# Cutting a weight load into pieces by rows: three uneven cuts taken away, one other cut put in

## The chip, the cores and the metric

The kernel runs on one core of one Trainium2 chip. The metric is the device time of one execution in microseconds; lower is better. Three executions of the kernel before took 427.69, 428.08 and 428.46 us, so the median is 428.08 us. A further execution was recorded by the hardware profiler; what is said below about engines, waits and transfers comes from that one.

## The reference, cut to what matters

The kernel computes sparse causal attention and then mixes its output in the frequency domain. In short:

```
attn = softmax(mask(q k^T / 8)) v          # 8 batches, 8 heads, 576 positions, 64 columns
x = attn, heads side by side                # [8, 576, 512]
X = rfft(x along the positions), modes 0..63
Yr = X.re @ w_r[m] - X.im @ w_i[m]          # one 512 x 512 complex matrix for each mode m
Yi = X.re @ w_i[m] + X.im @ w_r[m]
u = x + irfft(Y)
out = u + relu(u @ w_ch)                    # float32
```

The matrices w_r and w_i are float32 [64, 512, 512]: 64 MB each. Every element of them is read from memory once and used for 8 batches only. The page counts 162.83 MB read from memory in all.

## The kernel before, in words

**The stream of weights.** The work is cut along the 512 input columns into two halves of 256, and the modes are taken in pairs. One *fetch* brings, for one half and two neighbouring modes, the real part (256 rows of w_r for two modes, 1 MB of float32) into partitions 0 to 63 of a tile and the imaginary part (the same of w_i) into partitions 64 to 127. Each of the two is one DMA, issued by POOL, that converts float32 to float16 on its way: 64 rows (partitions) x 2 modes x 2048 numbers. In the profile it is `DMA_DIRECT2D wt<-in_moe_w_r_dram` or `...w_i_dram` on line 186, 512 KB as written.

`ORDER` (lines 150 and 151) lists 128 pairs (half, mode); entry i with even i stands for a fetch, so there are fetches i = 0, 2, ... 126. I call a fetch by i and its two DMAs 62r and 62i, 64r and 64i, and so on. The last two fetches (124 and 126) are made of four DMAs each, one for each part and mode (line 190, 256 KB as written).

**Pieces.** `UNEVEN` (line 152) names fetches whose real part is not one DMA of 64 rows but several of fewer rows, in the order given, over neighbouring partitions (lines 179 to 184; the issue is on line 182). Before, fetch 64 is cut into 25, 12 and 27 rows, fetch 80 into 6, 54 and 4, and fetch 96 into 10 and 54. The imaginary part is always whole. The total of bytes is the same with any cut.

**What orders the transfers.** The schedule is written out by hand (`manual_schedule`), so the instructions of each engine run in the order of the program. `w_fetch` is called where a mode pair has been used (lines 607 and 637), and its DMAs go on POOL's queue. The tiles come from a pool of five (`NWBUF`, line 27), so a fetch also waits until the matmuls of the pair five fetches back are done. In the list of POOL's instructions, its DMAs take one of eight semaphores in turn, and each waits for the DMA that used the same semaphore last, eight DMAs earlier. So up to eight of POOL's DMAs are under way at a time.

**What uses the weights.** `mode_pair` (lines 585 to 612, matmuls on line 597) multiplies by a pair once both its parts have landed. The last 16 modes of half 0 go through `mode` (lines 614 to 647, matmuls on line 630), one mode at a time, between pieces of other work: `renew` (lines 948 to 961), which folds spectra that are done into rows that were kept. When mode 127 of the order has been used, the last spectra are turned (lines 1042 to 1053) and the rows of the output are made and written (lines 1056 to 1081); nothing of that can start earlier for the last spectra.

**The stages.** From 0 to about 95 us the strided heads' attention runs beside loads of q, k and v; from about 95 to 195 us the local heads' attention runs between the first mode pairs of half 1; from about 195 us on there are only mode pairs, the product with w_ch and the turns of the attention output beside them; from about 392 us on all inputs are there and the output is made.

Of the kernel before, what the change touches and what calls it, by code (L numbers as in the profile page):

```python
# [56 lines left out]
def kernel(  # L57
# [91 lines left out]
    SPLIT1, SPLIT0 = 56, 48  # L149
    ORDER = [(1, m) for m in range(SPLIT1)] + [(0, m) for m in range(SPLIT0)]  # L150
    ORDER += [(1, m) for m in range(SPLIT1, NM)] + [(0, m) for m in range(SPLIT0, NM)]
    UNEVEN = {64: (25, 12, 27), 80: (6, 54, 4), 96: (10, 54)}
    w_tiles = []
    w_chs = {}
    w_ch = big.tile([128, 4, DM], F16, name="w_ch")
# [1 line left out]
    def w_fetch(n=1):  # L157
        for _ in range(n):
# [9 lines left out]
            for ri, src in enumerate((moe_w_r, moe_w_i)):  # L168
# [8 lines left out]
                if ri and not m:  # L177
                    ones = [1]
                elif i in UNEVEN and not ri:
                    a = 0  # L180
                    for n in UNEVEN[i]:
                        nc.gpsimd.dma_start(dst[a : a + n], rows[a : a + n])
# [930 lines left out]
```

## Time and profile before

| what | value |
|---|---|
| three executions, median (lowest to highest) | 428.08 us (427.69 to 428.46) |
| profiled execution, first to last instruction | 426.7 us |
| what the median has on top of that span | 1.4 us |
| busy: PE / DVE / ACT / POOL | 81% / 55% / 51% / 26% of the span |
| packets of POOL's DMAs, share of 16 DMA engines' time | 96.2% |
| 512 KB weight DMAs, median from issue to landing | 18.8 us (w_i), 17.7 us (w_r) |
| the eight pieces on line 182, issued | 218.3 to 300.0 us, 15.3 to 19.0 us to landing |
| last weight DMA issued, landing | 382.3 us, 9.6 us later |

How it is read: the page gives busy shares over the whole span, but a share near 100% says which resource is full, not which part of it ends last. The 16 DMA engines work side by side, each on its own share of every DMA, and a DMA has landed only when the last of them is done with it. The trace keeps a record of each packet (start, duration, size, queue), so one can also ask how far apart the 16 engines are. The chain of waits, followed back from the end, says which of all this the end waited for.

### The profile page before, as it was taken

How to read it: one execution, taken by the hardware profiler on the slowest of the kernel's cores; microseconds unless marked ns; L12 is line 12 of the kernel's file. 1: busy time of each engine (PE TensorE's matmuls, PEld its weight loads, DVE VectorE, ACT ScalarE, POOL GpSimd, SP SyncE). 2: the span in 40 equal slices, each digit the busy share in tenths (PEclk: the TensorE clock that was granted, in tenths of full speed). 3: DMA queues.
4: the chain of work that ended last, by engine and by line, in shares of the span. 5: the costliest groups of instructions: out<-in, count | busy, mean ns of one | idle time of the engine just before them, and what ended most of it. 6: DMA issues, size and time to landing. Idle time of an engine off the chain costs nothing.

```text
span 426.7 us, 9768 instructions
## 1 busy us (share of the span) xinstructions
PE 346.4 (81%) x4167; PEld 208.2 (49%) x4167; DVE 234.7 (55%) x466; ACT 218.3 (51%) x390; POOL 110.7 (26%) x196
## 2 busy tenths in 40 slices
PE   2977878769999698889768788878788867889993
PEld 2866767554656365566433344435444423445330
DVE  3788778851355154356113246746676354655884
ACT  1687678643656356556642235423442444443872
POOL 8332333322423222222222322222232222210000
PEclk9999899967999689999995889989999979989997
DMA  8999999999999999999999999999999999995698
GB/s 150 210 212 212 213 213 213 211 211 211 214 213 213 213 213 215 212 214 215 210 214 211 213 214 213 210 213 215 212 213 214 213 213 214 214 212 105 244 355 287
DMA packets 30938, 91.62 MB, mean 215 GB/s; under 512 B 4464, under 2 KB 5232, under 8 KB 30896
## 3 DMA queue, kind: packets, MB, share of 16 engines
q0 software_dynamic: 25168, 81.28, 96.2%
q1 hardware_dynamic: 4976, 9.13, 5.9%
q10 hardware_dynamic: 752, 0.61, 0.5%
q8 instruction: 32, 0.52, 0.5%
q14 instruction: 10, 0.08, 0.0%
HBM read 162.83 MB, written 9.44 MB: 404 GB/s over the span
## 4 chain that ended last, share of the span: by engine, by line
DMA 47%; PE 29%; DVE 14%; ACT 5%; issue 3%; DVEq 0%; POOL 0%; ACTq 0%; POOLq 0%
DMA wt<-in_moe_w_i_dram 38%; DMA wt<-in_moe_w_r_dram 7%; PE y L597 5%; DVE xb L241 3%; DVE kz L283 3%; PE p L987 2%; ACT X L251 2%; PE sc L532 2%; PE tp L413 2%; PE sc L459 1%; PE p L1001 1%; PE y L532 1%; PE p L760 1%; DVE yy L752 1%; DVE rec L240 1%
## 5 line engine op out<-in xcount | busy, mean ns | idle before, releaser
L597 PE MATMUL y<-wt,X 128*32 128x512 f16 (+1 forms) x448 | 70.9, 430 | 20.1 <-DMA wt<-in_moe_w_i_dram 20.1
L186 POOL DMA_DIRECT2D wt<-in_moe_w_r_dram x59 | 34.7, 588 | 126.4 <-PE y L597 56.3
L186 POOL DMA_DIRECT2D wt<-in_moe_w_i_dram x60 | 35.4, 590 | 68.3 <-DMA wt<-in_moe_w_i_dram 44.4
L597 PEld LDWEIGHTS <-X 128*32 128x32 f16 (+1 forms) x448 | 28.1, 140 | 39.4 <-DMA wt<-in_moe_w_i_dram 18.6
L727 DVE COPY xo<-tp 128x512 f16<-128x512 f16 x32 | 22.1, 691 | 36.8 <-PE tp L725 36.8
L726 ACT ACTIVATE v<-sc 128x512 f16<-128x512 f32 x32 | 19.1, 597 | 44.2 <-PE sc L717 44.2
L717 PE MATMUL sc<-w_cp,xT 128*128 128x512 f16 x128 | 36.9, 410 | 1.9 <-DVE xT L690 1.9
L489 ACT ACTIVATE PL<-sc 128x480 f16<-128x480 f32 (+1 forms) x48 | 27.0, 578 | 21.3 <-PE sc L475 21.0
L241 DVE TENSOR_TENSOR xb<-av,rec 90x256 f16<-90x256 f32 (+2 forms) x80 | 36.0, 450 | 2.8
L240 DVE RECIPROCAL rec<-av 90x4 f32<-90x4 f32 (+2 forms) x80 | 14.6, 183 | 39.3 <-PE av L504 28.2
L251 ACT ACTIVATE yr<-y 128x512 f16<-128x512 f32 x28 | 16.7, 597 | 36.8 <-PE y L597 35.6
L961 DVE TENSOR_TENSOR xo<-p,xo 128x1024 f16<-128x1024 f32 x16 | 19.6, 1225 | 21.7 <-PE p L760 21.7
L420 DVE COPY qT<-tp 128x576 f16<-128x576 f16 x16 | 11.9, 752 | 34.7 <-PE tp L413 34.7
L251 ACT ACTIVATE v<-p 128x1024 f16<-128x1024 f32 x16 | 16.4, 1023 | 23.1 <-PE p L760 23.1
L378 ACT ACTIVATE PL<-sc 90x360 f16<-90x360 f32 (+1 forms) x48 | 22.7, 490 | 7.0 <-PE sc L371 6.4
L251 ACT ACTIVATE v<-tp 128x640 f16<-128x640 f16 (+1 forms) x24 | 19.0, 807 | 11.8 <-PE tp L447 9.3
L413 PE MATMUL tp<-cI_s,ring 64*64 64x64 f16 x864 | 22.4, 197 | 2.7 <-DVE qT L420 2.4
L459 PE MATMUL sc<-cMl_s,cI_s 128*128 128x480 f16 (+1 forms) x48 | 19.4, 405 | 4.5 <-ACT PL L489 2.9
L276 PE MATMUL tp<-cI_s,ring 72*128 72x72 f16 x256 | 15.4, 207 | 8.7 <-DMA ring<-in_v_dram 7.1
L413 PEld LDWEIGHTS <-ring 64*64 64x64 f16 x864 | 17.5, 110 | 9.4 <-issue 5.4
L251 ACT ACTIVATE kz<-tp 64x360 f16<-64x360 f16 (+1 forms) x32 | 18.9, 592 | 6.2 <-PE tp L413 5.2
L1013 ACT ACTIVATE rl<-p 128x1024 f32<-128x1024 f32 (+1 forms) x19 | 18.4, 979 | 5.7 <-PE p L1001 3.1
(142 smaller groups left out, 737.9 us busy)
## 6 DMA issues: line engine op xcount, KB each, us to landing
wt<-in_moe_w_i_dram POOLq DMA_DIRECT2D x60, 512.0 KB, 18.8
wt<-in_moe_w_r_dram POOLq DMA_DIRECT2D x59, 512.0 KB, 17.7
out_dram<-osb SPq DMA_DIRECT2D x15, 512.0 KB, 3.4
ring<-in_v_dram POOLq DMA_DIRECT2D x8, 288.0 KB, 13.4
ring<-in_q_dram POOLq DMA_DIRECT2D x8, 288.0 KB, 13.6
ring<-in_k_dram POOLq DMA_DIRECT2D x8, 288.0 KB, 13.1
ring<-in_v_dram POOLq DMA_DIRECT2D x3, 512.0 KB, 14.8
ring<-in_q_dram POOLq DMA_DIRECT2D x3, 512.0 KB, 14.8
```

The lines of the kernel that those rows point to most:

```text
L186: nc.gpsimd.dma_start(dst, rows)
L241: nc.vector.tensor_tensor(out=dst, in0=val.rearrange("p h (q c) -> p h c q", c=4), in1=rec[0:n, 0:pieces] .to_broadcast((n, pieces, 64)) . ...
L251: nc.scalar.activation(out=out, in_=in_, func=ACTF.Copy)
L378: nc.scalar.activation(out=PS[0:n, ds(POFF[t], 4 * n)], in_=scp[0:n, 0 : 4 * n], func=ACTF.Exp, scale=SCALE,)
L413: nc.tensor.transpose(tp[ds(64 * hp, 64), ds(64 * i, 64)], qn[ds(64 * hp, 64), ds(64 * (9 * g + i), 64)], idn[ds(64 * hp, 64), ds(64 * hp, ...
L459: nc.tensor.matmul(scp[:, 0 : n * times].rearrange("p (h x) -> p h x", h=times), idn, mask_rows("cMl", n, times), start=True, stop=False,)
L489: nc.scalar.activation(out=dst, in_=src, func=ACTF.Exp, scale=SCALE)
L597: nc.tensor.matmul(yp[ds(a, 32), :], Xh[half][pr, c].rearrange("p b r (h m) -> p (b r h) m", h=2)[:, :, mm % 32], wt[pr, XC[c], :], start= ...
L717: nc.tensor.matmul(vp, xT[:, ch], w_chs["cp"][:, ch, :], start=(ch == 0), stop=(ch == 3),)
L726: nc.scalar.activation(out=v0, in_=vp, func=ACTF.Copy)
L727: nc.vector.tensor_copy(out=xo.rearrange("p (h q c) -> p h q c", h=2, c=4), in_=tp[:, 0:512].rearrange("p (h c q) -> p h q c", h=2, c=4),)
L961: nc.vector.tensor_tensor(out=xo, in0=up[:, 0:n], in1=xo, op=AluOp.add)
```

## The change

The dictionary `UNEVEN` is replaced. Fetches 64, 80 and 96 (half 0, modes 8, 24 and 40) are no longer cut: the real part of each becomes one DMA of 64 rows on line 186. Fetch 98 (half 0, modes 42 and 43), the next after 96, has its real part cut into five DMAs of 15, 14, 13, 12 and 10 rows.

```diff
     ORDER += [(1, m) for m in range(SPLIT1, NM)] + [(0, m) for m in range(SPLIT0, NM)]
-    UNEVEN = {64: (25, 12, 27), 80: (6, 54, 4), 96: (10, 54)}
+    UNEVEN = {98: (15, 14, 13, 12, 10)}
     w_tiles = []
```

POOL's queue has one row fewer: eight pieces become three whole DMAs, and one whole DMA becomes five pieces. As all later DMAs of POOL take their semaphores in turn, those get other numbers. The order of the instructions of PE, ACT, DVE and SP stays as it was, but for the semaphores they wait on.

## The prediction

> **What bounds the kernel now.** I read the page's slices first, then the chain of waits, then the timeline where the last weights arrive, then the packet records.
>
> ```profile
> DMA  8999999999999999999999999999999999995698
> ...
> q0 software_dynamic: 25168, 81.28, 96.2%
> ...
> DMA wt<-in_moe_w_i_dram 38%; DMA wt<-in_moe_w_r_dram 7%; PE y L597 5%; DVE xb L241 3%; DVE kz L283 3%; PE p L987 2%; ACT X L251 2%; PE sc L532 2%; PE tp L413 2%; PE sc L459 1%; PE p L1001 1%; PE y L532 1%; PE p L760 1%; DVE yy L752 1%; DVE rec L240 1%
> ```
>
> The DMA row stands at 9 until slice 36, so POOL's queue (96.2%) keeps all 16 DMA engines at work until the inputs are in; and 45% of the chain that ended last are weight DMAs. Next, the chain in order of time, near the last weights:
>
> ```profile
> 337.54 19.90 DMA wt<-in_moe_w_i_dram
> 357.44 0.28 issue
> 357.73 19.38 DMA wt<-in_moe_w_i_dram
> 377.10 0.14 issue
> 377.24 0.64 PE y L630 x16
> ```
>
> The DMA issued at 357.73 (120i) lands at 377.1 and PE starts 0.14 us later. After that PE is the chain, mode after mode, up to the last:
>
> ```profile
> 391.87 0.59 PE L992 MATMUL p<-xo,cI_s 128*128 128x512 f16 x2
> 392.09 0.73 PEld L630 LDWEIGHTS <-wt 128*128 128x128 f16 x16
> 392.31 0.64 PE L630 MATMUL y<-X,wt 128*128 128x16 f16 x16
> ```
>
> The last weight DMA is issued at 382.31 and lands 9.6 us later, at 391.9; PE loads from it at 392.09. So at the end transfer and PE arrive within 0.2 us of each other. What follows (392.3 to 426.7) is made of work that starts there. The end therefore moves with the moment at which the *slowest* DMA engine is done with the weights.
>
> **How far apart the engines are.** The packet records have no engine number, but POOL's packets follow each other without a gap: the next 4 KB packet starts 305 ns after the last, and at the end of each DMA an engine writes a 4 B packet, which costs 21 ns. A whole DMA is 8 packets on each engine; one engine's 4 B packets come 2457.5 ns apart (1239 ns for the last eight DMAs, of 4 packets). 16 such sequences can be followed from 225 us to the end. Each moves only where an instruction fetch (16 KB, queue q8) takes the engine for about 1.1 us, or an 8 KB one for 0.33 us. Their last 4 B packets come at 386.0 to 391.6 us, 389.4 in the mean: the slowest engine is 2.2 us behind the mean.
>
> The pieces of before show how rows go to engines. A piece runs on the largest number of engines up to 16 that divides its rows: 25 rows on 5 engines (10 packets each), 12 on 12 (2), 27 on 9 (6), 54 on 9 (12), 6 on 6, 4 on 4, 10 on 10 (2). Each piece begins at the engine after the last one of the piece before, around the ring of 16. An engine that has no rows writes as many 4 B packets as the others have data, 6 ns each. Numbering the engines from the first of the 25-row piece, the three cut DMAs together give an engine this many packets, where 24 would be even. "62i done" is the last moment that the change cannot touch; "end" is the last 4 B packet; the last two columns are worked out below.
>
> ```
> engines  packets  62i done (us)             end, before (us)          shift   end, after
> 0        26       229.1                     387.2                     -0.75   386.5
> 1-4      30       228.8 229.3 230.5 231.2   388.1 390.0 390.1 391.6   -1.95   386.2 388.0 388.2 389.7
> 5,6      22       231.8 232.4               389.0 390.4               +0.44   389.4 390.9
> 7,8      32       228.8 229.3               388.8 389.2               -2.55   386.2 386.7
> 9        22       231.5                     389.9                     +0.44   390.3
> 10-12    18       231.8 232.8 233.3         388.7 390.1 390.8         +1.64   390.3 391.7 392.4
> 13-15    18       229.5 232.8 233.0         386.0 389.7 390.2         +1.64   387.6 391.3 391.8
> ```
>
> (Which row a sequence belongs to follows from its packets in the three cut DMAs; within a row the order is by 62i.) What is to be seen: engines 10 to 15 are the late ones at 62i (mean 232.2, against 229.8 for 0 to 4), and the cuts of before give just them 6 packets fewer.
>
> **The change, part by part.**
>
> *Whole real parts for 64, 80, 96.* Every engine then has 24 packets there. Shift of an engine: packets x 304.6 ns, less its empty 4 B packets (22, 18, 26, 16, 26, 30, 30 down the table; about 2 after) x 6 ns, less 21 ns for one DMA fewer. Engines 10 to 15: 6 x 304.6 = +1.83, -0.17, -0.02: +1.64 us. Engines 7 and 8: -8 x 304.6 = -2.44, -0.08, -0.02: -2.55 us.
>
> *Five pieces for 98.* By the same two habits 15, 14, 13, 12 and 10 rows take 15, 14, 13, 12 and 10 engines with one row (2 packets) each. They are 64 places on a ring of 16: 4 for every engine, 8 packets, as from a whole DMA. So this cut shifts nobody; its four more DMAs (4 x 21 ns, at most 0.1 us) are already in the shift.
>
> *Last engine.* From the table the latest end goes from 391.61 (an engine of 1-4) to 390.81 + 1.64 = 392.45 (one of 10-12): **+0.84 us**. Lower bound: that engine's clean time is 233.33 at 62i + 59 whole DMAs (145.0) + the cut one (2.56) + eight short ones (9.91) = 390.8; it came 1.68 us late at 94i, of which a 16 KB fetch at 277.5 explains about 1.1; the other 0.5 falls in 271 to 278 us, where the cut of fetch 80 was being written and many packets took 330 to 570 ns instead of 324. If that goes with the cut, the last end is some 391.9, **+0.25 us**. I take +0.84, the measured delay of the same engine, since the fetch itself took 1.2 us there and nothing shows that the empty packets caused the rest.
>
> *End of the kernel.* 120i lands 0.84 later and PE begins at 378.1 instead of 377.24. From 377.55 to 380.97 the granted clock is 0.5; PE loses 0.31 us at full and 0.55 at half speed, 0.6 in all, so the mode before the last is done at some 393.1 instead of 392.5. The last DMA lands at 392.7 instead of 391.9, so PE's load moves from 392.09 to 392.8: +0.75 us at the last mode. All after it follows. Span 426.7 + 0.75 = 427.4; the median has 1.4 us on top of the span: **428.9 us**.
>
> *Costed at nothing.* POOL's issues: 0.59 us for a whole DMA, 0.57 to 0.71 for a piece, one fewer in all; they are hidden because a DMA is issued 15 to 19 us ahead of its landing. Semaphores: five pieces take five of the eight places, so fewer bytes are queued behind them. When the slowest engine ends 94i it has 96r, 96i and the pieces ahead, 3 x 2.46 = 7.4 us, and 98i is issued then; an engine ahead by 5.8 to 6.5 us (307.4 against 313.2 to 313.9 by the table) may run dry for about a microsecond, but it has 5 us to spare and is not the one waited for. Without that cover each microsecond of dry queue would be one at the end. PE's waits before 392 us: its pairs wait on two parts as before; at 94i the slowest engine would be up to 0.9 us earlier (no heavy cut yet behind it), but PE waits for weights again and again from 342 to 377 us (1.2 to 2.9 us each), so that is lost.
>
> *A rule against the rows.* The trace shows engines taking the next DMA's packet 21 ns after the last. The Trainium skill, "DMA: Bandwidth & Descriptors", section "Anatomy of one DMA", gives about 2.0 us fixed for each DMA on this path. By that, one DMA fewer would be -2 us; with eight under way this trace shows no such cost in the stream. The same page, "Why a DMA increments its semaphore by 16 and not by 1", tells the divisor rule that the pieces show, but also an exception by which 100 partitions go on engines 0 to 14, each copy starting at 0. By the exception the five pieces would give ten engines 10 packets and one none, up to +0.6 us on a late engine, 429.5 in all; the pieces of before don't follow it.
>
> **Rivals.**
>
> 1. *Balance lost, tail follows* (forecast): 428.9; with the bounds 428.3 to 429.0 from the DMA alone.
> 2. *The loss is no loss* (no change): the 0.5 us went with the bursts of empty packets, and PE's half-clock stretch swallows the rest: +0.1 to +0.3, 428.3. For it: packets of 500 to 570 ns around the bursts. Against: 391.8 of another engine stays.
> 3. *Instruction fetches fall elsewhere* (faster). Three of the four latest engines owe 1.1 us each to one fetch after 235 us (298.6, 317.7, 332.6), the fourth the one at 277.5. If the new order of POOL's rows moves them to engines that have time, the last end is 390.8, -0.8 us: 427.2. It decides once all four are spared, since any one of them left is over 391.3. Against: PE, ACT and DVE have the same instructions in the same order, and fetches follow from those.
> 4. *Clock* (slower still). Half-clock stretches come in steps of 3.41 us. The chain from 392 to 419 has PE pieces of 0.54 between others and no such stretch; one there, or a longer one at 377, adds up to 1.7 us: 430.5.
> 5. *Not what it says*: pieces of 15, 14, 13 rows are not in the trace; if they don't follow the ring, a late engine gets up to 10 packets instead of 8: +0.6, 429.5.
>
> **How the numbers follow.** Chances: forecast 0.50, rival 2 0.18, rival 3 0.16, rival 4 0.10, rival 5 0.06. A measurement of this kernel can tell about 0.2% from no change, 0.86 us (427.2 to 428.9). The forecast sits on the upper edge; a little over two thirds of it I count as over, since a later 120i moves work behind it that I have counted at half clock. Slower: 0.35 + 0.10 + 0.05 = 0.50; same: 0.15 + 0.15 + 0.02 = 0.32; faster: 0.15 and 0.03 from rival 2, 0.18. The range takes in rival 3 with 0.2 us below it and rival 4 but for its far end: 427.0 to 430.2.
>
> **What would show it.** Right: 94i's 4 B packets no later than before, but a spread of the last 4 B packets of over 6 us (5.6 before), the last at 392.0 to 392.5; five pieces of 2 packets on 15, 14, 13, 12, 10 engines; 120i landing at 377.4 to 378. Wrong: a last landing at or before 391.9; engines with other than 8 packets in 98r; a chain that doesn't go through 120i or the last DMA.

## The result, and the profile after

| | runs | median (lowest to highest), us |
|---|---|---|
| before, on the same chip | 22 | 427.96 (427.29 to 429.16) |
| changed | 22 | 428.56 (428.02 to 430.55) |

The ratio is 1.0018, 95% interval 1.0011 to 1.0026. The kernel is 0.6 us slower by its medians. The prediction said 428.9, and slower by about 0.8. The profiled execution of the changed kernel took 428.65 us, its span is 426.9.

The page of the changed kernel, the lines that answer to those of before (slices of the DMA engines, POOL's queue, the chain that ended last by line):

```profile
DMA  8999999999999999999999999999999999995698
...
q0 software_dynamic: 24800, 81.28, 96.1%
...
DMA wt<-in_moe_w_i_dram 47%; PE y L597 5%; DMA wt<-in_moe_w_r_dram 4%; PE p L987 2%; PE p L1001 1%; DVE yy L752 1%; PE sc L717 1%; PE sc L459 1%; PE p L992 1%; PE tp L413 1%; PE y L532 1%; PE sc L475 1%; ACT X L251 1%; PE u L992 1%; PE av L496 1%
```

The DMA engines are as full as before, digit for digit, and the bytes are the same; 368 packets are gone, and all of them are 4 B packets (384 empty ones in the three old cuts against 32 in the new one, and 16 fewer at the end of a DMA). Weight DMAs are now 51% of the chain against 45%. The chain in order of time says why (start us, us, what):

```profile
357.28 19.45 DMA wt<-in_moe_w_i_dram
376.73 0.28 issue
377.01 12.33 DMA wt<-in_moe_w_i_dram
389.34 0.14 issue
389.48 0.64 PE y L630 x16
390.11 1.51 PE p L987 x4
391.62 0.85 PE p L992 x2
392.47 0.49 PE y L630 x16
```

Before, the chain left the DMAs at 377.1 and was nearly all PE from there on. Now it follows one more weight DMA, which lands at 389.34. PE's timeline around it, in the changed kernel (start us, us; in brackets the idle time ahead of the row and what ended it):

```profile
389.48 0.64 PE L630 MATMUL y<-X,wt 128*128 128x16 f16 x16 [0.94 <-DMA wt<-in_moe_w_i_dram]
389.95 1.67 PE L987 MATMUL p<-v,cI_s 128*128 128x512 f16 x4
391.41 1.06 PE L992 MATMUL p<-xo,cI_s 128*128 128x512 f16 x2
392.26 0.68 PE L630 MATMUL y<-X,wt 128*128 128x16 f16 x16
```

The last mode is multiplied at 392.26; before, in the profile that the prediction read, at 392.31. So in this pair of executions the last mode came no later, though the medians differ. What comes behind it does: the two matmuls of line 992 take 1.06 us instead of 0.59, because the stretch in which TensorE's clock is granted at half speed (0.5) now lies at 390.2 to 393.6 us (before at 377.6 to 381.0).

Of the fourteen profiles in this document these two alone have a half-speed stretch between 370 and 420 us. In eleven of the other twelve the chain comes to the last mode through the last weight DMA. This is its end in a kernel without any cut (no_cut, below):

```profile
382.21 9.63 DMA wt<-in_moe_w_i_dram
391.84 0.14 issue
391.97 0.65 PE y L630 x16
```

The exception is a second profile of the kernel before (before_again), in which PE itself comes last. Its last mode is multiplied at 391.73 us; without a cut that happens at 391.97 and 392.01, in the two further profiles of the changed kernel at 391.99 and 392.50.

**One profile is one draw.** In 227 of 232 runs the time stood 1.73 to 2.08 us above the span (median 1.79 of all); the other five, 2.4 to 3.0 us above it, are all of one kernel, old_and_five. The span of before has a median of 426.1 us over the 87 runs that were made beside the experiments, and the profiled execution of 426.7 was among the slowest fifth. The changed kernel's median span is 426.7 over 45 runs. So the two profiles differ by 0.2 us where the medians differ by 0.6, and half a microsecond can't be read from one pair of traces. The packet records, which show where each DMA engine stands, are more use.

In the records of the changed kernel the last 4 B packet of POOL's DMAs comes at 391.54 us (before 391.61). The 16 engines end in two groups: eight at 387.3 to 388.5, eight at 390.0 to 391.5. Before they were spread from 386.0 to 391.6.

### The profile page after: what moved, and what is told of

Its sections match the earlier page's. It is cut to its first block, busy times and chain, and to the rows that moved or that the text cites. A ratio compares the mean times of both kernels' runs of the same rounds, so it can differ in the third digit from the quotient of the medians.

```text
span 426.9 us, 9766 instructions
## 1 busy us (share of the span) xinstructions
PE 344.6 (81%) x4167; PEld 207.2 (49%) x4167; DVE 234.8 (55%) x466; ACT 218.3 (51%) x390; POOL 109.8 (26%) x195
## 4 chain that ended last, share of the span: by engine, by line
DMA 52%; PE 19%; DVE 4%; ACT 2%; issue 2%; POOL 0%; DVEq 0%; ACTq 0%
DMA wt<-in_moe_w_i_dram 47%; PE y L597 5%; DMA wt<-in_moe_w_r_dram 4%; PE p L987 2%; PE p L1001 1%; DVE yy L752 1%; PE sc L717 1%; PE sc L459 1%; PE p L992 1%; PE tp L413 1%; PE y L532 1%; PE sc L475 1%; ACT X L251 1%; PE u L992 1%; PE av L496 1%
## 5 line engine op out<-in xcount | busy, mean ns | idle before, releaser
L597 PE MATMUL y<-wt,X 128*32 128x512 f16 (+1 forms) x448 | 69.3, 422 | 21.2 <-DMA wt<-in_moe_w_i_dram 20.9
L186 POOL DMA_DIRECT2D wt<-in_moe_w_r_dram x61 | 35.8, 588 | 132.5 <-PE y L597 41.2
```

The lines of the kernel that those rows point to most:

```text
L186: nc.gpsimd.dma_start(dst, rows)
L597: nc.tensor.matmul(yp[ds(a, 32), :], Xh[half][pr, c].rearrange("p b r (h m) -> p (b r h) m", h=2)[:, :, mm % 32], wt[pr, XC[c], :], start= ...
```

## The experiments

Each kernel is the one before with line 152 alone changed. Runs were made in three groups, each with runs of the kernel before on the same chip (medians 427.79, 427.94 and 428.03 us). The first is before_again, no_cut, old_and_five and more_for_late; the second after_again, four_even, many_even and less_for_late; the third no_cut_b, after_c, five_early and two_fives. "Last packet" is the last 4 B packet of POOL's DMAs in the profiled execution. "Lost" is what is left over of the 180 us between 200 and 380 us, as a mean over the 16 engines, when each packet is counted at its usual length (305 ns for 4 KB); it is good for differences between kernels.

| line 152 | median us (runs) | ratio, 95% interval | span | last packet | lost us |
|---|---|---|---|---|---|
| as before (before_again) | 427.99 (12) | 1.0006, 0.9997 to 1.0016 | 426.2 | 391.25 | 0.4 |
| no cut (no_cut) | 428.22 (12) | 1.0007, 0.9999 to 1.0016 | 426.5 | 391.51 | 0.4 |
| no cut (no_cut_b) | 428.30 (12) | 0.9997, 0.9981 to 1.0013 | 426.5 | 391.55 | 0.4 |
| as changed (after_again) | 428.29 (11) | 1.0014, 1.0003 to 1.0024 | 426.3 | 391.56 | 1.0 |
| as changed (after_c) | 428.40 (12) | 1.0002, 0.9988 to 1.0016 | 427.0 | 392.06 | 0.9 |
| old cuts and the five pieces (old_and_five) | 428.31 (12) | 1.0016, 1.0003 to 1.0028 | 426.2 | 391.38 | 0.9 |
| four equal pieces at 98 (four_even) | 428.92 (11) | 1.0019, 1.0009 to 1.0030 | 427.1 | 392.05 | 0.6 |
| four equal pieces at 90 to 100 (many_even) | 429.81 (6) | 1.0038, 1.0025 to 1.0052 | 428.5 | 393.79 | 3.5 |
| five pieces at 66 instead (five_early) | 428.66 (12) | 1.0005, 0.9992 to 1.0019 | 427.0 | 392.09 | 1.5 |
| five pieces at 82 and 98 (two_fives) | 428.70 (12) | 1.0008, 0.9993 to 1.0022 | 427.0 | 392.17 | 1.1 |
| more rows for the late engines (more_for_late) | 431.19 (6) | 1.0073, 1.0059 to 1.0087 | 428.7 | 393.82 | 1.2 |
| fewer for the late ones (less_for_late) | 429.45 (5) | 1.0031, 1.0019 to 1.0043 | 427.9 | 392.97 | 0.3 |

The third group's intervals are wide (its 35 runs of before reach from 427.3 to 430.9), so the small differences are read from all runs together. Before: 427.94 (121 runs). No cut: 428.25 (24). Changed: 428.53 (45). The differences of these medians, with intervals from resampled runs: no cut less before +0.31 us (0.21 to 0.47), changed less no cut +0.27 us (0.02 to 0.43), changed less before +0.59 us (0.34 to 0.76). The runs come from several chips, which these intervals don't count. Chip by chip, no cut is 0.43 and 0.27 us above the runs of before beside it, the changed kernel 0.60, 0.35 and 0.37. Only the third chip ran both: there the changed kernel is 0.10 us above no cut (-0.24 to 0.47).

### The two halves of the change

before_again changes nothing:

```diff
     UNEVEN = {64: (25, 12, 27), 80: (6, 54, 4), 96: (10, 54)}
```

> The kernel before once more, for a second profile of it. Both theories: ratio 1.000, within 0.0007. Theory of balance: the engines' last 4 B packets again spread over 5 to 6 us, the last one at 391 to 392 us, and the time of the profiled execution moves with the last one (about 1 us for 1 us). Theory of the small pieces: says nothing of it.

It came out at 427.99 us, 1.0006 (0.9997 to 1.0016), as expected. Its engines end at 386.0 to 391.2 us, another order of the same spread: the last packet of one and the same program moves by 0.4 us from one profile to another. This is the yardstick for everything below.

no_cut, and later no_cut_b, take the old cuts away and put none in:

```diff
-    UNEVEN = {64: (25, 12, 27), 80: (6, 54, 4), 96: (10, 54)}
+    UNEVEN = {}
```

> No fetch is cut. Theory of balance (where the rows go sets the time, cutting itself is free): as the changed kernel, 1.0010 to 1.0026 of before, since 15+14+13+12+10 rows give every engine the same. Theory of the small pieces (five small DMAs hold five of the eight places, the queue runs dry behind them, and that is the loss): no loss, 0.999 to 1.0005 of before.

> No fetch is cut, beside the changed kernel and two others. Theory A (the small DMAs of a cut cost time of their own, because they take places among the eight that may be under way, so that fewer bytes are queued and the engines that are ahead run dry): 1.0004 to 1.0012 of the time of before, and below the changed kernel by 0.2 to 0.5 us. Theory B (the five pieces cost nothing; all that the change costs is the balance that the old cuts gave): the same as the changed kernel within 0.15 us.

The first, at 1.0007, lies between the ranges of its two theories. The second, at 0.9997 in the group with the wide intervals, lies below all of them; it is 0.10 us under the changed kernel beside it, which is what theory B asked for (within 0.15 us), but the interval of -0.24 to 0.47 doesn't shut out theory A (0.2 to 0.5). Together they are 0.31 us slower than before. The last packets of the two profiles agree (391.51 and 391.55), and the engines end in two groups, as in the changed kernel: without the old cuts, eight of them stay, in the mean, 3 to 4 us behind the other eight to the end. So the old cuts were worth something, but about 0.3 us. That these 0.3 us are the last engine's isn't seen directly: the last packets, two profiles each, are 0.1 us apart (mean 391.53 without a cut, 391.43 before), less than the 0.4 us by which those of one program differ.

old_and_five keeps the old cuts and puts the five pieces in beside them:

```diff
-    UNEVEN = {64: (25, 12, 27), 80: (6, 54, 4), 96: (10, 54)}
+    UNEVEN = {64: (25, 12, 27), 80: (6, 54, 4), 96: (10, 54), 98: (15, 14, 13, 12, 10)}
```

> The three cuts of before and the five pieces at fetch 98. Theory of balance: as before, 0.9993 to 1.0007. Theory of the small pieces: as the changed kernel or worse, 1.0010 to 1.0026.

At 1.0016 (1.0003 to 1.0028) its times are some 0.5 us longer than before, with the old balance in place. But five of its twelve runs have 2.4 to 3.0 us on top of their spans instead of 1.8, for a reason that no profile here shows. Its spans have a median of 426.2 us, as before has over all its runs (0.2 us more than the 426.0 of the runs beside it, with an interval of -0.1 to 0.75). So this run doesn't show that the five pieces cost anything between the first instruction and the last. In its profile they hold back the engines that are ahead: the 16 end within 2.4 us of each other, and the last packet, at 391.38, lies between the two of before (391.25 and 391.61).

after_again and after_c are the changed kernel, as the measure for the others of their groups:

```diff
-    UNEVEN = {64: (25, 12, 27), 80: (6, 54, 4), 96: (10, 54)}
+    UNEVEN = {98: (15, 14, 13, 12, 10)}
```

> The changed kernel once more, beside the others of this row. Both theories: 1.0010 to 1.0026 of before. If only the place of the rows counted, it would equal the kernel without cuts (1.0007 of before, interval 0.9999 to 1.0016); if the five pieces cost something of their own, it stays some 0.3 us above that.

> The changed kernel once more, as the measure for the other three. Both theories: 1.0010 to 1.0024 of the time of before; last 4 B packet of POOL's DMAs at 391.3 to 391.8 us; about 0.6 to 1.0 us of each DMA engine's time lost between 200 and 380 us, most of it near 316 to 324 us.

1.0014 and 1.0002: the first as expected, the second below the range that was expected, which its wide interval (0.9988 to 1.0016) still overlaps.

### Is it the slowest engine that counts?

more_for_late cuts so that the engines that are late get more rows, and less_for_late so that they get fewer:

```diff
-    UNEVEN = {64: (25, 12, 27), 80: (6, 54, 4), 96: (10, 54)}
+    UNEVEN = {64: (5, 50, 9), 80: (1, 56, 7)}
```

> Cuts that work against the balance: fetch 64 in 5, 50 and 9 rows, fetch 80 in 1, 56 and 7. Numbered as in the prediction, engines 5, 6 and 9 to 13 get 4 packets more than even (14 gets 2 more), 0 to 4 four fewer, 7 and 8 two fewer, 15 six fewer. Theory of balance: the late engines end 4 x 0.305 = 1.2 us later than with no cut, so 1.8 us over before, 1.0035 to 1.005. Theory of the small pieces: six pieces far apart, as before has eight, 0.999 to 1.001.

```diff
-    UNEVEN = {64: (25, 12, 27), 80: (6, 54, 4), 96: (10, 54)}
+    UNEVEN = {64: (7, 56, 1), 80: (9, 50, 5), 96: (22, 14, 28)}
```

> Cuts fitted to the ends of the engines in the kernel without cuts: fetch 64 in 7, 56 and 1 rows, 80 in 9, 50 and 5, 96 in 22, 14 and 28. Engines 0 to 4 get 6 packets more than even, 7, 8 and 15 get 4 more, 5, 6 and 14 four fewer, 9 to 13 six fewer. Theory of balance: the late engines end 1.2 to 1.8 us earlier than with no cut, the last 4 B packet at 389.9 to 390.6 us, 0.997 to 0.999 of before, unless the cutting itself eats it. If cutting costs and the balance counts for little: 1.001 or more.

more_for_late ends late, by more than it should: the last packet at 393.82 us instead of 391.5 without a cut, 2.3 us later where 1.2 was expected, and the time 2.9 us longer than without a cut (1.0073 of before, expected 1.0035 to 1.005). The four packets more account for 1.2 us of it; 0.8 us of engine time more are lost in its packets than without a cut, and why is open. Its chain (start us, us, what):

```profile
384.54 9.59 DMA wt<-in_moe_w_i_dram
394.12 0.14 issue
394.26 0.65 PE y L630 x16
```

The last weight DMA lands at 394.12 and PE begins 0.14 us later; PE has no part in the chain between 365 and 394 us.

less_for_late was to be faster (0.997 to 0.999) and is slower too, at 1.0031, though fifteen of its engines end at or before 390.5 us. One, which the plan had counted among those with time, had been late already and got more on top: behind the cut of fetch 80 it is 1.7 us behind all the others, and an instruction fetch at 276.85 us takes it 1.1 more. It ends at 393.0. The expectation's other branch (1.001 or more if cutting costs) gives the same sign, but only 0.3 us are lost here, less than in any other kernel. What the DMA engines move in the last stretches of this kernel (columns: the stretch, its length, busy time of PE, PEld, DVE, ACT and POOL with their instructions, granted clock, DMA share, GB/s):

```profile
384.00:388.00 4.00, 4.00 (x53) 2.33 (x49) 2.78 (x3) 2.27 (x3) 0.20 (x1) 1.00 1.00 198
388.00:392.00 4.00, 3.30 (x45) 1.90 (x44) 2.81 (x4) 1.62 (x2) 0.00 (x0) 1.00 0.29 56
392.00:396.00 4.00, 3.04 (x33) 1.67 (x31) 0.34 (x2) 0.45 (x1) 0.00 (x0) 1.00 0.02 3
```

The queue moves less from 388 to 392 us than the changed kernel does (56 against 76 GB/s): most engines are done. From 392 on it moves 3 GB/s, that is 3 x 4 us = 12 KB, three packets of one engine. The landing waits for them, and the time with it. This is the clearest sight of the rule that the slowest engine counts: the mean of the 16 ends is no worse here (389.1 us, before 389.4), and the kernel is slower.

In all fourteen profiles, from the least last packet (391.25) to the largest (393.82), the span is 34.7 to 35.3 us more than it, so the end follows the slowest engine one for one.

### What do the five pieces cost, and why?

Two reasons could be thought of: the empty packets of engines without rows, or the eight places. four_even cuts fetch 98 into pieces of 16 rows. Each piece runs on all 16 engines, so that nothing is uneven and no packet is empty. many_even does that at six fetches.

```diff
-    UNEVEN = {64: (25, 12, 27), 80: (6, 54, 4), 96: (10, 54)}
+    UNEVEN = {98: (16, 16, 16, 16)}
```

> The real part of fetch 98 in four pieces of 16 rows, nothing else cut: every engine has one row of each piece, no engine is without data, so no empty packets, and four of the eight places hold a quarter each. Theory of balance: as with no cut, 1.0000 to 1.0015 of before. Theory of the shallow queue (small DMAs in the eight places let it run dry): as the changed kernel, 1.0012 to 1.0026. If it is the empty packets of uneven pieces that cost: as with no cut.

```diff
-    UNEVEN = {64: (25, 12, 27), 80: (6, 54, 4), 96: (10, 54)}
+    UNEVEN = {90: (16, 16, 16, 16), 92: (16, 16, 16, 16), 94: (16, 16, 16, 16),
+              96: (16, 16, 16, 16), 98: (16, 16, 16, 16), 100: (16, 16, 16, 16)}
```

> Six fetches in a row (90 to 100) with the real part in four pieces of 16 rows. A place holds on the average 0.4 of a DMA, so some 8 us of work are queued for the last engine and less than that for one that is ahead. Theory of balance: still as with no cut, 1.0000 to 1.0015 of before, since nobody gets more. Theory of the shallow queue: six times the dose, 1.005 or more.

four_even came out as expected for a shallow queue (1.0019); against no cut, over all its runs, that is 0.67 us (0.06 to 1.05). many_even, at 1.0038, missed both ranges: 1.56 us over no cut (1.04 to 2.3), far more than nothing, but about twice four_even for six times the dose. So pieces cost without an empty packet and with every engine getting the same: neither the empty packets nor uneven rows are needed for it. Stretches of the kernel without a cut, of the changed one, and of many_even (columns as above; look at the last):

```profile
312.00:316.00 4.00, 2.25 (x22) 1.11 (x20) 3.63 (x6) 2.26 (x4) 1.18 (x2) 0.97 1.06 213
316.00:320.00 4.00, 4.00 (x23) 1.90 (x22) 1.71 (x5) 0.89 (x2) 0.09 (x1) 0.60 1.06 213
320.00:324.00 4.00, 3.48 (x34) 2.08 (x33) 2.44 (x5) 1.50 (x3) 1.09 (x2) 1.00 1.06 213
```

```profile
312.00:316.00 4.00, 2.25 (x15) 0.91 (x12) 3.28 (x7) 1.47 (x3) 0.93 (x2) 0.89 1.06 209
316.00:320.00 4.00, 4.00 (x27) 2.03 (x26) 1.39 (x3) 1.39 (x3) 1.57 (x4) 0.69 1.05 201
320.00:324.00 4.00, 3.48 (x31) 1.91 (x30) 2.44 (x5) 1.00 (x2) 2.17 (x4) 1.00 1.07 211
```

```profile
312.00:316.00 4.00, 3.35 (x20) 1.90 (x22) 2.72 (x6) 0.60 (x1) 1.25 (x3) 0.69 1.05 187
316.00:320.00 4.00, 3.83 (x30) 1.89 (x27) 1.57 (x4) 1.79 (x3) 1.32 (x3) 0.88 1.15 184
320.00:324.00 4.00, 3.65 (x34) 2.15 (x33) 2.47 (x6) 0.60 (x1) 2.75 (x5) 1.00 1.14 193
```

Without a cut the queue moves 213 GB/s in all three. The changed kernel falls to 201 in the stretch behind its pieces: (4 + 12 + 2) / 213 x 4 us = 0.34 us of an engine's time in the mean; by the same three stretches its two other profiles lose 0.69 and 0.51. many_even falls to 184 to 193 in each. The DMA share (the number before the last) stays at 1.05 or rises; the bytes show it. What grows is the length of packets: between 313 and 322 us two or three 4 KB packets take more than 327 ns without a cut, 28 to 36 in the three profiles of the changed kernel, 89 in four_even and 206 in many_even.

POOL's timeline in the changed kernel shows where this comes from: the issue of the last piece, then 98i, 100r, 100i, 102r, 102i, 104r and 104i.

```profile
310.58 0.55 POOL L182 DMA_DIRECT2D wt<-in_moe_w_r_dram  x1 [1.91 <-DMA wt<-in_moe_w_r_dram]
313.05 0.60 POOL L186 DMA_DIRECT2D wt<-in_moe_w_i_dram  x1 [1.92 <-DMA wt<-in_moe_w_i_dram]
315.68 0.59 POOL L186 DMA_DIRECT2D wt<-in_moe_w_r_dram  x1 [2.02 <-DMA wt<-in_moe_w_r_dram]
318.06 0.58 POOL L186 DMA_DIRECT2D wt<-in_moe_w_i_dram  x1 [1.79 <-DMA wt<-in_moe_w_i_dram]
319.28 0.58 POOL L186 DMA_DIRECT2D wt<-in_moe_w_r_dram  x1 [0.64 <-PE y L597]
319.85 0.60 POOL L186 DMA_DIRECT2D wt<-in_moe_w_i_dram  x1
320.56 0.59 POOL L186 DMA_DIRECT2D wt<-in_moe_w_r_dram  x1
321.13 0.60 POOL L186 DMA_DIRECT2D wt<-in_moe_w_i_dram  x1
```

Up to 318 us an issue comes every 2.4 us: each waits until the DMA eight places earlier has landed, and those were whole ones. At 313.05, when 98i goes out, the places ahead hold 96r, 96i and five pieces that make one DMA between them. As soon as the pieces land, four DMAs go out within 2.5 us: the queue is filled again. In between, the engines that are ahead had little or nothing. From the end of 96i to that of 98i the eight engines ahead take 4.92 and 4.94 us in the mean of the two profiles without a cut, and 5.34, 5.31 and 5.04 in the three of the changed kernel, where four more DMAs explain 0.08. The eight that are late take 5.11 and 5.06 without a cut, and 5.36, 5.00 and 5.06 in the changed kernel: they lose a quarter of a microsecond in one profile and nothing in two.

five_early moves the five pieces to fetch 66, where the engines are closer together; two_fives has them at 82 and at 98.

```diff
-    UNEVEN = {64: (25, 12, 27), 80: (6, 54, 4), 96: (10, 54)}
+    UNEVEN = {66: (15, 14, 13, 12, 10)}
```

> The five pieces (15, 14, 13, 12, 10 rows) at fetch 66 in place of 98; no other cut. At 62i the engines are 4.5 us apart, at 94i about 6 us. Theory A: engines ahead run dry less, lost DMA time near the pieces 0.1 to 0.4 us for each engine instead of 0.6, so 1.0005 to 1.0013 of the time of before, between no cut and the changed kernel. Theory B: as no cut. If the cost of the pieces has nothing to do with how far apart the engines are, it is that of the changed kernel, 1.0014 to 1.0020.

```diff
-    UNEVEN = {64: (25, 12, 27), 80: (6, 54, 4), 96: (10, 54)}
+    UNEVEN = {82: (15, 14, 13, 12, 10), 98: (15, 14, 13, 12, 10)}
```

> The five pieces at 82 and at 98 both; no other cut. Theory A: twice the cost of one set on top of no cut, 1.0020 to 1.0032 of the time of before, with two stretches of lost DMA time, near 268 to 280 us and near 316 to 324 us; last 4 B packet at 391.8 to 392.6 us. Theory B: as no cut, 1.0004 to 1.0012.

five_early's ratio (1.0005) falls at the edge of theory A's range, but what that theory said of it did not happen: it lost more DMA time, not less, and is as slow as the changed kernel (428.66 us), 0.36 us (0.03 to 0.71) over the no cut beside it. Its stretches, and POOL's timeline there:

```profile
240.00:244.00 4.00, 2.98 (x17) 1.58 (x17) 1.39 (x3) 1.27 (x2) 2.16 (x4) 0.64 0.94 170
244.00:248.00 4.00, 2.79 (x25) 1.59 (x24) 1.72 (x4) 1.87 (x3) 2.49 (x5) 1.00 1.04 199
```

```profile
234.14 0.60 POOL L186 DMA_DIRECT2D wt<-in_moe_w_i_dram  x1 [1.99 <-DMA wt<-in_moe_w_i_dram]
237.10 0.59 POOL L186 DMA_DIRECT2D wt<-in_moe_w_r_dram  x1 [2.36 <-DMA wt<-in_moe_w_r_dram]
241.84 0.58 POOL L186 DMA_DIRECT2D wt<-in_moe_w_i_dram  x1 [4.14 <-issue]
242.41 0.60 POOL L186 DMA_DIRECT2D wt<-in_moe_w_r_dram  x1
...
245.26 0.65 POOL L186 DMA_DIRECT2D wt<-in_moe_w_i_dram  x1
```

Here POOL stood still for 4.14 us just when the queue was shallow, and then sent seven whole DMAs in 4 us. The profile names no reason; the place among the eight that it needed had come free at 238.7 us, 3.1 us before the issue. The kernel without a cut has such a pause too, from 229 to 234 us:

```profile
228.69 0.59 POOL L186 DMA_DIRECT2D wt<-in_moe_w_i_dram  x1 [1.59 <-DMA wt<-in_moe_w_i_dram]
234.18 0.60 POOL L186 DMA_DIRECT2D wt<-in_moe_w_r_dram  x1 [4.90 <-issue]
```

There it costs nothing (213 to 214 GB/s), with up to eight whole DMAs of 2.46 us each queued. A queue of small DMAs has less cover. (43 + 15) / 213 x 4 us = 1.09 us is lost in the mean, and the engines come out closer together, about 389 to 392.1 us at the end: it is the ones ahead that lost most. How much of the 1.09 us is the pause's and how much the pieces' isn't separated.

two_fives was to cost twice one set by theory A, and doesn't: 428.70 us, 0.40 us (0.10 to 0.56) over the no cut beside it. Its ratio of 1.0008 is in theory B's range, but B said that pieces cost nothing. At 280 to 284 us, behind the first set, it falls to 180 GB/s, without a pause of POOL. At the second set it hardly falls:

```profile
280.00:284.00 4.00, 1.88 (x21) 1.18 (x19) 2.22 (x5) 0.60 (x1) 2.91 (x5) 1.00 1.05 180
...
316.00:320.00 4.00, 4.00 (x22) 1.90 (x21) 1.85 (x5) 0.75 (x2) 1.36 (x3) 0.57 1.06 210
320.00:324.00 4.00, 3.48 (x34) 1.98 (x32) 2.44 (x5) 1.64 (x3) 2.14 (x4) 1.00 1.06 208
```

This fits a loss that limits itself: once the engines that are ahead have been set back, a second shallow stretch finds less to take. That was not tried by itself. Neither of the two theories stated for it is right as it stood: in this kernel the pieces cost something on top of no cut, and the second set adds little.

## Why the prediction was right, and which terms were off

**Direction and sum: right, the sum partly by luck.** Slower by 0.75 us was forecast, 0.59 (0.34 to 0.76) was measured over all runs. The term that was to give all of it came to 0.31; the other 0.27 stands, as far as the runs can tell, with a term that was put at nothing. Two errors of opposite sign met. The forecast's time of 428.9 was 0.37 above the 428.53 of all runs: 0.16 from this size and as much from the base, the rest from rounding. The base was the profiled execution's span plus 1.4 us, 428.1, where before has 427.94. The 1.4 was the median's distance from a span that was not of a median run; the distance between a run's time and its own span is 1.8.

**The slowest engine sets the end: right.** more_for_late and less_for_late show it from two sides.

**Last engine +0.84: over twice too large.** No cut costs 0.31 us (0.21 to 0.47), near the lower bound of the term (+0.25). The term moved one late engine's end by the packets that it lost in the cuts. It took as given that this engine would also meet the same delays, 1.68 us at 94i. In the changed kernel 94i has landed by 312.8 us, against 314.5 before, so that engine didn't meet them, and the last packet comes at 391.5 to 392.1 in its three profiles, 391.5 in those without a cut. The prediction had named the 0.5 us in the stretch of fetch 80's cut, where the late engine lost time, and left it in. That all of the difference is those 0.5 us isn't shown: the last packet of one program moves by up to 0.5 us between profiles.

**Five pieces, cost at nothing: too low, as far as can be told.** Changed less no cut is +0.27 us (0.02 to 0.43) over all runs, but 0.10 (-0.24 to 0.47) on the one chip that ran both, and the spans of old_and_five show no such cost. For the five pieces at fetch 98 alone the size stays open, and nothing is not shut out. That pieces can cost is shown by larger doses and other places: two_fives 0.40 us and five_early 0.36 over the no cut beside them, many_even 1.56 over all runs of no cut. The prediction did name the mechanism, with the place and the engines: five of eight places, the engines ahead dry "for about a microsecond", and "each microsecond of dry queue would be one at the end" without cover. All three profiles of the changed kernel do move fewer bytes behind the pieces (194 to 201 GB/s at 316 to 320 us, against 213 and 214 without a cut), and it is mainly the engines ahead that lose. If the prediction got something wrong here, it is that the cover of the late ones is complete: in one profile of three they lose 0.25 us there. How a dry stretch of the engines that are ahead reaches those that are behind stays open. The late engines of the three changed profiles end at most 0.6 us later than without a cut, mean 391.72 against 391.53 for the last packet, which is less than one program's own scatter. The long packets behind the pieces (28 to 36, against 2 or 3) may be the link; that was not tried.

**Tail +0.75, by way of the half clock: not as described.** 120i landed at 376.73, not later than before; the half-speed stretch moved from 377.6 to 390.2 us, behind the last weights, where the prediction had placed none. The last weights landed at 391.8, 0.3 us behind the last 4 B packet, which by the prediction's own test (a last landing at or before 391.9) counts against this step; in the two further profiles it was 391.8 and 392.4. So does its sign of a spread of over 6 us: it is 4.2 (387.3 to 391.5), 3.7 and 4.3 in the three profiles. The working has a slip as well: it has the mode before the last done at 392.5 us, where the profile has that one at 390.54 to 391.18 and PE free for the last mode at 392.5; the sum goes by the last landing and isn't touched. The step was read from one pair of executions, and one pair can't carry it: a half-speed stretch between 370 and 420 us stands in no other profile. Without a cut, and in the two further profiles of the changed kernel, the last mode waits for the last weight DMA, the other path that the prediction named, and comes 0.2 to 0.8 us later than in before_again.

**Where the pieces go: right.** At 313 to 320 us runs of two empty 4 B packets are found, and the page's count of packets agrees with sixteen of them, 1 + 2 + 3 + 4 + 6: what 15, 14, 13, 12 and 10 engines with 2 packets each leave over. The count doesn't say which engines those are; the times do. An engine with 10 packets would take 0.6 us more over 98r and 98i than one with 8, and an engine with none 2.4 us less; paired in order of their ends, the sixteen engines of after_c take 4.9 to 5.2 us, and none of the three profiles has an engine under 4.8. So the rival in which pieces don't follow the ring falls. The Trainium skill, "DMA: Bandwidth & Descriptors", section "Why a DMA increments its semaphore by 16 and not by 1", gives an exception for some copies (an equal number of partitions, rounded up, on each engine in turn until they are used up); it isn't seen here. The page's main rule, the largest divisor up to 16, is: by it the old cuts leave 384 empty packets and the new one 32, as many as the counts above ask for.

**Per-DMA price.** The same page's section "Anatomy of one DMA" gives about 2 us fixed for a DMA on this path. many_even issues 18 DMAs more than no cut and takes 1.6 us longer (429.81 against 428.25), 0.09 us for each; two_fives issues eight more and takes 0.4, 0.05 for each. The measurement decides: 2 us for each is not what more DMAs cost in this stream, where the next packet starts 21 ns after the last 4 B packet of the DMA before.

**Other rivals.** That the balance lost is no loss stands between: +0.1 to +0.3 was its price, 0.31 the measured one. It is the better account of the cuts in size, though its reason (the 0.5 us gone with the bursts of empty packets) isn't shown. Fetches that fall elsewhere and a longer half clock are not needed; each profile has 32 instruction fetches of 16 KB, and most stand within 3 us of the same place in another kernel's profile; on which engine each falls wasn't followed.

**Against a better version.** No cut and the changed kernel are both slower than before; two tries at other amounts were slower still. Nothing that was run beats the kernel before.

## What to carry to other kernels

When a queue keeps all DMA engines full to the end, ask which of the 16 ends last, not how busy they are: here more bytes on the late engines cost at least in full, and an earlier end of fifteen brought nothing. When DMAs share a fixed number of places, count the microseconds of transfer that the places hold; cutting a transfer into pieces shrinks that cover, even if every engine gets the same bytes. For differences of half a microsecond in 428, size a term from several executions, since a single profile may be half a microsecond from its own median.

## What the runs showed that was not expected

- An engine without rows in a piece still writes as many packets as the others, of 4 B and 6 ns each; the 384 in the old cuts come to 0.14 us of an engine's time in the mean.
- With equal bytes on each (no cut) the 16 engines end over 5 us apart. Each instruction fetch of 16 KB takes one engine for about 1 us (its packet 0.9 to 1.2), and as long as the queue is full nothing here evens that out.
- Running dry evens the engines out, by holding back those ahead: the spread at the end is over 5 us without a cut and about 3 us with five pieces at fetch 66, and the kernel is no faster for it.
- POOL can stand for 4 to 5 us, some 3 us of them with no cause in the profile (229 to 234 us without a cut). With whole DMAs queued this was free; in five_early it met a shallow queue, and 1.1 us of the mean engine's time went (0.6 behind the first set of two_fives, without a pause).
- Of the three kernels with the most runs the one without a cut scatters least: the middle half of the runs of before lies within 0.65 us (427.66 to 428.31), of the changed kernel within 0.63 (428.18 to 428.81), of the kernels without a cut within 0.25 (428.17 to 428.41).
